# Pooled attention and mixture of depths: keys on every second partition, exponentials in four tiles, row broadcasts moved ahead

## The chip, the cores and the metric

The kernel runs on one core of a Trainium2 chip. The metric is device time in microseconds (us) of one execution, as the median of several runs. The core has five engines with a queue each: PE (TensorE, with PEld for its weight loads), DVE (VectorE), ACT (ScalarE), POOL (GpSimd) and SP (SyncE, which issues most transfers here). Each works through its own queue in order and waits for the others by semaphores.

## What is computed

The input q, k and v have shape 8 x 8 x 576 x 64 (batch, heads, tokens, head size). Keys and values are averaged over groups of 8 tokens, so each head has 72 keys:

```
k_p = k.reshape(B, H, 72, 8, D).mean(axis=3); v_p likewise
attn = softmax(q @ k_p^T / sqrt(D)); x = attn @ v_p       # x as (B, 576, 512)
scores = x @ w_gate                                       # one per token
top = the 128 tokens of each batch with the highest score
out = x; out[top] += sigmoid(scores[top]) * (relu(x[top] @ w1) @ w2)
```

w1 is 512 x 1024 and w2 is 1024 x 512. Everything is float32.

## The kernel before

All the work is in `direct_path` (`general_path` is a second way that runs only when a flag says that a softmax sum left its range, which these inputs don't do). There are 8 batches. A batch has 3 steps (`u`, 24 in all), and a step has two chunks of 96 tokens.

**Loads.** SP's queue loads k and q as 128-partition tiles (L99, L103) and v as two tiles of four heads (`load_v`, L105 to L110), with the 72 keys on partitions 0 to 71, in one transfer of 64 partitions and one of 8. Batches 0 and 1 are loaded at the start, and batch b+2 while batch b is worked on.

**Pooling.** `pool_k` (L180, L181) and `pool_v` (L197 to L201) add neighbouring tokens. They run on POOL, apart from k of batch 0 and the second v tile of batch 0, which run on DVE. `k_trans` on DVE transposes k (L186) and makes the last addition (L190). `gate_v` on DVE (L205) puts v times w_gate, summed, into one more column of the pooled v. A further column holds the constant 8, so that the attention matmul also gives the softmax sum.

**A step.** `attend` (L244, PE) multiplies the exponentials of one chunk by the pooled v, `norm` (L256 to L262, DVE) divides by the sum, `scores` (L227, PE) makes the scores of the next step into four PSUM banks, and four ACT instructions (L232) take their exponentials into one tile `et`. `q_trans` (L215, DVE) transposes q for the step after that.

**Selection and MLP of a batch.** `row_bcast` (L304 on PE, L306 on ACT) copies a batch's 576 scores to all partitions, in two halves. `count` (six of them, L316, L318 and L320 on DVE) counts for each token how many are ahead of it. `one_hot` (L325, L327, DVE) and `gather` (L334 on PE, L336 to L342 on DVE and POOL) turn the ranks into the 128 rows, fetched by an indirect transfer. `gate` (L350 to L352 on ACT, POOL, DVE), `x_trans` (L357, L359), `hidden` (L369, L371) and `finish` (L381 to L383, and the scatter L385) make the MLP and add it.

**The order** is written out by hand. The loop at L455 issues, for each step, attend, norm, slot 1, scores, slot 2, attend, norm, q_trans and slots 3 to 7. The table at L401 to L431 says which job of which batch goes in which slot. With w the step after a batch's last, the batch's row broadcasts stand in slots 4 and 6 of step w, and its counts in slot 7 of steps w, w+1 and w+2. In the same step w stand the finish parts 1 and 2 of the batch two before (slots 3 and 5), `gate` and `x_trans` of the batch before (slots 2 and 7), and the pooling of k and of the first v tile of the next batch on POOL.

Of the kernel before, what the change touches and what calls it, by code (L numbers as in the profile page):

```python
# [7 lines left out]
FT = mybir.dt.float32  # L8
# [3 lines left out]
OP = mybir.AluOpType  # L12
AX = mybir.AxisListType
# [35 lines left out]
def direct_path(ctx, tc, q, k, v, moe_w_gate, moe_w1, moe_w2, moe_capacity, out, flag):  # L49
# [49 lines left out]
    def load_q(b):  # L101
        QR[b] = work.tile([128, TG, D], FT, name="qraw")
        nc.sync.dma_start(out=QR[b], in_=q[b].rearrange("h (g t) d -> (h g) t d", g=G))  # L103

    def load_v(b, g):  # L105
        x = work.tile([SP, HG, POOLW, D], FT, name="vraw", bufs=4)
        VR[b, g] = x
        src = v[b, HG * g : HG * (g + 1)].rearrange("h (p t) d -> p h (t d)", t=POOLW)
        for lo, hi in ((0, 64), (64, SP)):
            nc.sync.dma_start(out=x[lo:hi].rearrange("p h t d -> p h (t d)"), in_=src[lo:hi])  # L110

    load_k(0)
    load_q(0)
# [2 lines left out]

    wg = const.tile([SP, H, D], FT)
    nc.scalar.dma_start(out=wg.rearrange("p h d -> p (h d)"),  # L120
                        in_=bass.AP(tensor=moe_w_gate.tensor, offset=moe_w_gate.offset, ap=[[0, SP], [1, DM]]))
# [14 lines left out]
    vps = []  # L136
    for i in range(2):
        t = const.tile([SP, H, E], FT, name=f"vp{i}")
        nc.gpsimd.memset(t[:, :, D : D + 1], float(POOLW))
        nc.gpsimd.memset(t[:, :, D + 2 : E], 0.0)  # L140
        vps.append(t)
# [41 lines left out]
    def k_trans(b):  # L183

        half = work.tile([128, 2, 2 * G, R], FT, name="kh", bufs=1)
        nc.vector.transpose(out=half.rearrange("p j c r -> p r j c"),  # L186
                            in_=KS[b].rearrange("p r (j e) -> p r j e", j=2))
        KT[b] = work.tile([128, 2, 2, SP], FT, name="kt")
        x = half.rearrange("p j c r -> p (j c r)").rearrange("p (n two) -> p n two", two=2)
        nc.vector.tensor_tensor(out=KT[b].rearrange("p j s n -> p (j s n)"), in0=x[:, :, 0], in1=x[:, :, 1],  # L190
                                op=OP.add)

    def pool_v(b, g, eng):
        x = VR[b, g]
# [24 lines left out]

    def scores(u):  # L220
        b = u // NTH
        p = [bank(i, [SP, 4, 128]) for i in range(4)]
        for s in range(2):
            for j in range(2):
                for i in range(4):
                    r = slice(32 * i, 32 * i + 32)
                    nc.tensor.matmul(p[i][:, 2 * s : 2 * s + 2, 0:C], KT[b][r, j, s, :],  # L227
                                     QT[u][r, :, j, :, G * s : G * s + G],
                                     start=(j == 0), stop=(j == 1))
        ET[u] = work.tile([SP, H * 2, G, CT], FT, name="et")  # L230
# [6 lines left out]
    def attend(a):  # L237
        u, cc = divmod(a, 2)
        b = u // NTH
        p = psum.tile([C, 2, 512], FT, name="pA")  # L240
        for h in range(H):
            g, n = divmod(h, HG)

            nc.tensor.matmul(p[:, g, E * n : E * n + E], ET[u][:, 2 * h + cc].rearrange("p g t -> p (g t)"),  # L244
                             VP[b][:, h, :], start=True, stop=True)
        PA[a] = p[:, :, 0 : HG * E].rearrange("p g (n d) -> p g n d", d=E)

# [146 lines left out]
    def at(u, slot, *job):  # L394
        jobs.setdefault((u, slot), []).append(job)
# [442 lines left out]
```

## Time and profile before

| what | value |
|---|---|
| median of 3 runs | 322.35 us (321.96 to 323.08) |
| the profiled execution's own time | 325.23 us |
| its span, first to last instruction | 323.4 us |
| PE busy | 270.0 us (83%) |
| DVE busy | 192.0 us (59%) |
| POOL busy | 147.9 us (46%) |
| ACT busy | 103.1 us (32%) |

The profile is one execution. A line of a timeline gives the start and the length of an instruction or of a merged run of them, its line in the kernel, the tile written and the tiles read, and in brackets how long the engine had waited before it and for what. A chain of waits follows the work that ended last back to what released it. Busy shares are averages over stages with different limits, so each stage is read by itself.

### The profile page before, as it was taken

Reading aid. Unit: us, or ns where it says so; the run is one execution under the profiler, and the core shown is the slowest. Engines: PE = TensorE matmul, PEld = TensorE weight load, DVE = VectorE, ACT = ScalarE, POOL = GpSimd, SP = SyncE. Lnnn points to the kernel's source line nnn. Section 1 sums busy time; section 2 is a strip of 40 time slices with the busy share of each in tenths; the row PEclk is TensorE's granted clock in tenths of the full one; section 3 lists DMA queues with packets and bytes.
Section 4 is the critical chain, followed back from the end, with each engine's and each line's share of the span. In section 5 each row is a group of like instructions: output and inputs, shape, how many; then the busy total and the mean of one; then the engine's idle time right before and its main releaser. Section 6 shows DMA issues by size and latency. Waiting matters only on the chain.

```text
span 323.4 us, 6460 instructions
## 1 busy us (share of the span) xinstructions
PE 270.0 (83%) x2562; PEld 247.6 (77%) x2562; DVE 192.0 (59%) x604; ACT 103.1 (32%) x178; POOL 147.9 (46%) x182
## 2 busy tenths in 40 slices
PE   0368769963699999979999799969996999999890
PEld 0238658853489989968998699969996899989890
DVE  0985532897358638992699439962897367383000
ACT  1150332350422444242344054404541441221210
POOL 1269408901890077907491649345862120423111
PEclk9965755595757999995999599978998799999997
DMA  7999999999692286637651937021111121201001
GB/s 248 247 225 310 221 339 309 230 262 330 118 240 79 63 239 143 210 96 207 145 206 32 264 101 228 29 82 46 40 49 51 32 83 52 82 34 32 34 0 43
DMA packets 12954, 46.78 MB, mean 145 GB/s; under 512 B 1324, under 2 KB 1324, under 8 KB 10868
## 3 DMA queue, kind: packets, MB, share of 16 engines
q1 hardware_dynamic: 11552, 41.95, 47.1%
q0 software_dynamic: 1280, 4.20, 4.2%
q8 instruction: 22, 0.36, 0.5%
q10 hardware_dynamic: 84, 0.15, 0.3%
q14 instruction: 16, 0.13, 0.1%
HBM read 34.75 MB, written 11.53 MB: 143 GB/s over the span
## 4 chain that ended last, share of the span: by engine, by line
PE 51%; DVE 32%; DMA 8%; issue 3%; POOL 2%; ACT 1%; SPq 0%; POOLq 0%; ACTq 0%
PE pA L244 18%; PE bank L381 13%; PE bank L227 9%; PE bank L369 9%; DVE cmp L320 7%; DVE cmp L318 4%; DVE cmp L316 4%; DVE xs L258 4%; DMA vraw<-in_v_dram 4%; DVE qt L215 3%; DMA xr<-out_dram,idx 3%; DVE kh L186 2%; DVE kt L190 2%; DVE oh L327 1%; DMA out_dram<-xs 1%
## 5 line engine op out<-in xcount | busy, mean ns | idle before, releaser
L232 ACT ACTIVATE et<-bank 72x384 f32<-72x384 f32 x96 | 71.1, 900 | 123.3 <-PE bank L227 123.3
L244 PEld LDWEIGHTS pA<-vp,et 72*96 72x96 f32 x768 | 88.2, 202 | 16.4 <-issue 11.2
L244 PE MATMUL pA<-vp,et 72*96 72x96 f32 x768 | 95.3, 290 | 6.4 <-DVE vp L205 3.6
L227 PE MATMUL bank<-qt,kt 32*72 32x192 f32 x768 | 53.3, 422 | 18.2 <-DVE qt L215 12.3
L369 PE MATMUL bank<-xg,w 128*128 128x128 f32 x512 | 61.4, 280 | 1.5 <-ACT xg L359 1.5
L369 PEld LDWEIGHTS bank<-xg,w 128*128 128x128 f32 x512 | 59.8, 196 | 1.9 <-ACT xg L359 1.9
L381 PE MATMUL bank<-w,ht 128*128 128x176 f32 (+1 forms) x384 | 59.5, 309 | 0.0
L383 POOL TENSOR_TENSOR y<-y,xr 128x176 f32<-128x176 f32 (+1 forms) x24 | 13.2, 551 | 97.8 <-ACT y L382 97.7
L227 PEld LDWEIGHTS bank<-qt,kt 32*72 32x72 f32 x768 | 37.1, 181 | 27.0 <-DVE qt L215 12.3
L381 PEld LDWEIGHTS bank<-w,ht 128*128 128x128 f32 x384 | 55.9, 190 | 0.0
L197 POOL TENSOR_TENSOR vraw<-vraw 72x1024 f32<-72x1024 f32 x15 | 35.4, 2361 | 12.0 <-DMA vraw<-in_v_dram 11.9
L258 DVE TENSOR_TENSOR xs<-pA,rz 96x512 f32<-96x512 f32 x48 | 33.0, 686 | 1.7
L320 DVE SCALAR_TENSOR_TENSOR cmp<-sr,sc,before 96x96 bf16<-96x96 f32 x48 | 32.1, 669 | 0.3
L318 DVE TENSOR_SCALAR_CACHE_REDUCE cmp<-sr,sc 96x576 bf16<-96x576 f32 (+5 forms) x48 | 26.6, 554 | 9.4 <-ACT sr L306 9.4
L256 DVE TENSOR_SCALAR zall<-pA 96x8 f32<-96x8 f32 x48 | 7.5, 156 | 41.2 <-PE pA L244 41.2
L371 ACT ACTIVATE ht<-bank 128x384 f32<-128x384 f32 (+1 forms) x24 | 10.9, 455 | 41.9 <-PE bank L369 41.9
L382 ACT ACTIVATE y<-bank,g 128x176 f32<-128x176 f32 (+1 forms) x24 | 9.7, 403 | 42.1 <-PE bank L381 42.1
L215 DVE STREAM_TRANSPOSE qt<-qraw 128x768 f32<-128x768 f32 x24 | 23.1, 964 | 0.0
L352 DVE RECIPROCAL g<-g 128x1 f32<-128x1 f32 x8 | 1.3, 163 | 36.1 <-POOL g L351 36.1
L316 DVE TENSOR_SCALAR_CACHE_REDUCE cmp<-sr,sc 96x96 bf16<-96x96 f32 (+4 forms) x40 | 20.2, 505 | 0.9
L180 POOL TENSOR_TENSOR kraw<-kraw 128x1152 f32<-128x1152 f32 x7 | 18.5, 2636 | 2.5 <-DMA kraw<-in_k_dram 2.5
L198 POOL TENSOR_TENSOR vraw<-vraw 72x512 f32<-72x512 f32 x15 | 19.0, 1269 | 1.2
(70 smaller groups left out, 180.7 us busy)
## 6 DMA issues: line engine op xcount, KB each, us to landing
kraw<-in_k_dram SPq DMA_DIRECT2D x8, 1152.0 KB
qraw<-in_q_dram SPq DMA_DIRECT2D x8, 1152.0 KB
out_dram<-xs SPq DMA_DIRECT2D x24, 384.0 KB
vraw<-in_v_dram SPq DMA_DIRECT2D x16, 512.0 KB
w<-in_moe_w_dram SPq DMA_DIRECT2D x2, 2048.0 KB
vraw<-in_v_dram SPq DMA_DIRECT2D x16, 64.0 KB
wg<-in_moe_w_gate_dram ACTq DMA_DIRECT2D x1, 144.0 KB
xr<-out_dram,idx POOLq DMA_INDIRECT x8, 4.8
```

The source lines that it names most:

```text
L197: eng.tensor_tensor(out=x[:, :, 0:4, :], in0=x[:, :, 0:4, :], in1=x[:, :, 4:8, :], op=OP.add)
L198: eng.tensor_tensor(out=x[:, :, 0:2, :], in0=x[:, :, 0:2, :], in1=x[:, :, 2:4, :], op=OP.add)
L215: nc.vector.transpose(out=QT[u].rearrange("p cc j t c -> p t (cc j) c"), in_=QR[b].rearrange("p (t c) d -> p t (c d)", c=NC)[:, :, 2 * D * ...
L227: nc.tensor.matmul(p[i][:, 2 * s : 2 * s + 2, 0:C], KT[b][r, j, s, :], QT[u][r, :, j, :, G * s : G * s + G], start=(j == 0), stop=(j == 1))
L232: nc.scalar.activation(ET[u][:, 4 * i : 4 * i + 4].rearrange("p n g t -> p n t g"), p[i][:, :, 0:C].rearrange("p n (t g) -> p n t g", g=G) ...
L244: nc.tensor.matmul(p[:, g, E * n : E * n + E], ET[u][:, 2 * h + cc].rearrange("p g t -> p (g t)"), VP[b][:, h, :], start=True, stop=True)
L258: nc.vector.tensor_tensor(out=XS[b][:, c, :].rearrange("p (g n d) -> p g n d", g=2, d=D), in0=o[:, :, :, 0:D], in1=rz.rearrange("p (g n on ...
L316: nc.vector.tensor_scalar(cmp[:, 0 : c * C], row[:, 0 : c * C], s, None, op0=OP.is_ge, op1=OP.add, accum_out=CN[b][:, c, 0:1])
L318: nc.vector.tensor_scalar(cmp[:, c * C : S], row[:, c * C : S], s, None, op0=OP.is_gt, op1=OP.add, accum_out=CN[b][:, c, 1:2])
L320: nc.vector.scalar_tensor_tensor(cmp[:, 0:C], row[:, c * C : c * C + C], s, before, op0=OP.is_equal, op1=OP.mult, accum_out=CN[b][:, c, 2:3])
L369: nc.tensor.matmul(p[:, n, :], w1[:, d, 128 * f : 128 * f + 128], XG[b][:, d, :], start=(d == 0), stop=(d == DB - 1))
L381: nc.tensor.matmul(p, HT[b][:, f, :], w2[:, f, c], start=(f == 0), stop=(f == FB - 1))
```

## The change

v is loaded to every second partition: keys 0 to 63 go to partitions 0, 2, ..., 126 and keys 64 to 71 to partitions 1, 17, ..., 113. The partitions between hold zeros, so the tiles that carry keys all have 128 partitions: the pooled v (`vp`), the transposed keys (`kt`, now 128 columns with zeros between), the score banks and the exponentials. The zeros are written once at the start. The column of 8s must be 8 on the partitions with a key only, so it is built from an index tile. The last addition of `k_trans` becomes two. The exponentials go to four tiles in place of one. Both row broadcasts move to slot 3 and to other banks, the finish parts 1 and 2 to slots 5 and 6, the third count to step w, and the last count and `one_hot` to slot 3.

```diff
+    vraws = [const.tile([128, HG, POOLW, D], FT, name=f"vraw{i}") for i in range(4)]
+    for i, t in enumerate(vraws):
+        (nc.vector, nc.gpsimd)[i % 2].memset(t, 0.0)
     def load_v(b, g):
-        x = work.tile([SP, HG, POOLW, D], FT, name="vraw", bufs=4)
+        x = vraws[(2 * b + g) % 4]
...
-        for lo, hi in ((0, 64), (64, SP)):
-            nc.sync.dma_start(out=x[lo:hi].rearrange("p h t d -> p h (t d)"), in_=src[lo:hi])
+        x = x.rearrange("p h t d -> p h (t d)")
+        nc.sync.dma_start(out=x[0:128:2], in_=src[0:64])
+        nc.sync.dma_start(out=x[1:128:16], in_=src[64:SP])
...
-    wg = const.tile([SP, H, D], FT)
+    wg = const.tile([128, H, D], FT)
...
+    vps = [const.tile([128, H, E], FT, name=f"vp{i}") for i in range(2)]
+    kts = [const.tile([128, 2, 2, 128], FT, name=f"kt{i}") for i in range(2)]
+    for t in kts + vps:
+        nc.gpsimd.memset(t, 0.0)
+    keys = const.tile([128, SP], FT)
+    nc.gpsimd.iota(keys[:, 0:64], pattern=[[2, 64]], base=0, channel_multiplier=-1,
...
+    nc.gpsimd.iota(keys[:, 64:SP], pattern=[[16, 8]], base=1, channel_multiplier=-1,
...
+    eights = const.tile([128, 1], FT)
+    nc.vector.tensor_scalar(keys, keys, 0.0, float(POOLW), op0=OP.is_equal, op1=OP.mult)
+    nc.vector.tensor_reduce(out=eights, in_=keys, axis=AX.X, op=OP.add)
+    for t in vps:
+        nc.vector.tensor_scalar(t[:, :, D], t[:, :, D], eights, None, op0=OP.add)
...
-        nc.vector.tensor_tensor(out=KT[b].rearrange("p j s n -> p (j s n)"), in0=x[:, :, 0], in1=x[:, :, 1],
-                                op=OP.add)
+        nc.vector.tensor_tensor(out=y[:, :, 0:128:2], in0=x[:, :, 0:64, 0], in1=x[:, :, 0:64, 1], op=OP.add)
+        nc.vector.tensor_tensor(out=y[:, :, 1:128:16], in0=x[:, :, 64:SP, 0], in1=x[:, :, 64:SP, 1], op=OP.add)
...
-        p = [bank(i, [SP, 4, 128]) for i in range(4)]
+        p = [bank(i, [128, 4, 128]) for i in range(4)]
...
-        ET[u] = work.tile([SP, H * 2, G, CT], FT, name="et")
+        ET[u] = [work.tile([128, 4, G, CT], FT, name=f"et{i}") for i in range(4)]
...
-        p = bank(2 * half + 1, [C, n, C])
+        p = bank(half, [C, n, C])
...
-        at(w, 4, row_bcast, b, 0)
-        at(w, 6, row_bcast, b, 1)
+        at(w, 3, row_bcast, b, 0)
+        at(w, 3, row_bcast, b, 1)
         for c in range(NC):
-            at(w + (0 if last else (0, 0, 1, 1, 1, 2)[c]), 7, count, b, c)
-        at(w + (0 if last else 2), 7, one_hot, b)
+            at(w + (0 if last else (0, 0, 0, 1, 1, 2)[c]), 7 if last or c < 5 else 3, count, b, c)
+        at(w + (0 if last else 2), 7 if last else 3, one_hot, b)
...
-        at(w + 6, 3, finish, b, 1, 0)
-        at(w + 6, 5, finish, b, 2, 2)
+        at(w + 6, 5, finish, b, 1, 2)
+        at(w + 6, 6, finish, b, 2, 3)
```

## Rows read from the trace of the kernel before

**Rows 1.** Chain of waits, pieces: start, length, engine, tile, line
```profile
113.08 0.97 DVE oh L327
...
144.56 0.97 DVE oh L327
...
178.77 0.96 DVE oh L327
...
190.13 2.22 PE bank L381 x16
...
193.08 0.83 DVE cmp L318 x2
...
247.09 0.96 DVE oh L327
```

**Rows 2.** Timeline of DVE in one turn (start, length; in brackets the wait before)
```profile
155.99 0.96 DVE L215 STREAM_TRANSPOSE qt<-qraw 128x768 f32<-128x768 f32 x1
...
158.90 0.81 DVE L318 TENSOR_SCALAR_CACHE_REDUCE cmp<-sr,sc 96x576 bf16<-96x576 f32 x1 [1.94 <-ACT sr L306]
...
159.75 3.34 DVE L320 SCALAR_TENSOR_TENSOR cmp<-sr,sc,before 96x96 bf16<-96x96 f32 x1
...
168.68 1.24 DVE L190 TENSOR_TENSOR kt<-kh 128x288 f32<-128x288 f32 x1
...
172.33 0.31 DVE L320 SCALAR_TENSOR_TENSOR cmp<-sr,sc,before 96x96 bf16<-96x96 f32 x1
...
176.90 0.37 DVE L205 TENSOR_REDUCE vp<-vraw 72x4 f32<-72x256 f32 x1
```

**Rows 3.** Timeline of POOL in the same turn
```profile
159.47 1.10 POOL L385 DMA_INDIRECT out_dram<-y,idx  x1 [0.29 <-POOL y L383]
160.59 2.38 POOL L197 TENSOR_TENSOR vraw<-vraw 72x1024 f32<-72x1024 f32 x1
...
168.33 1.27 POOL L198 TENSOR_TENSOR vraw<-vraw 72x512 f32<-72x512 f32 x1
```

**Rows 4.** Timeline of PE: batch 0's gather, then the same turn and the next
```profile
78.14 0.32 PE L334 MATMUL bank<-auxb,oh 96*128 96x5 bf16 x6 [6.08 <-DVE oh L327]
...
160.13 1.54 PE L227 MATMUL bank<-qt,kt 32*72 32x192 f32 x32
...
179.78 0.32 PE L334 MATMUL bank<-auxb,oh 96*128 96x5 bf16 x6 [2.44 <-DVE oh L327]
...
182.74 2.85 PE L227 MATMUL bank<-qt,kt 32*72 32x192 f32 x32
```

**Rows 5.** Busy time by stretch: us, PE, PEld, DVE, ACT, POOL, PEclk, DMA, GB/s
```profile
100.90:145.30 44.40, 41.52 (x452) 39.20 (x451) 34.11 (x110) 17.43 (x30) 19.98 (x23) 1.00 0.49 140
...
179.40:186.20 6.80, 6.42 (x58) 5.36 (x59) 2.10 (x9) 0.53 (x1) 4.89 (x8) 0.50 0.92 242
186.20:213.50 27.30, 25.18 (x264) 24.08 (x263) 21.98 (x64) 12.13 (x22) 14.61 (x14) 1.00 0.41 120
```

**Rows 6.** Timeline of ACT, the exponentials of a step
```profile
185.67 2.98 ACT L232 ACTIVATE et<-bank 72x384 f32<-72x384 f32 x4 [7.89 <-PE bank L227]
```

**Rows 7.** Busy time by stretch at the start, columns as in rows 5
```profile
6.00:8.00 2.00, 0.00 (x0) 0.00 (x0) 0.55 (x1) 0.00 (x0) 0.00 (x0) 1.00 0.99 410
...
10.00:12.00 2.00, 0.00 (x0) 0.00 (x0) 1.97 (x3) 0.00 (x0) 0.00 (x0) 1.00 1.03 199
```

**Rows 8.** Timelines of POOL and DVE at the start
```profile
1.45 0.29 POOL L140 MEMSET vp<- 72x240 f32 x1
...
21.69 2.75 POOL L180 TENSOR_TENSOR kraw<-kraw 128x1152 f32<-128x1152 f32 x1 [2.48 <-DMA kraw<-in_k_dram]
...
22.00 2.72 DVE L201 TENSOR_TENSOR vraw<-vp,wg 72x256 f32<-72x256 f32 x1
```

**Rows 9.** Groups of weight loads between 160 and 179 us (busy, mean ns)
```profile
L369 PEld LDWEIGHTS bank<-xg,w 128*128 128x128 f32 x64 | 7.3, 192 | 0.0
...
L227 PEld LDWEIGHTS bank<-qt,kt 32*72 32x72 f32 x64 | 2.4, 137 | 0.4 <-issue 0.3
```

More of the change, by code (lines that the diff above doesn't have):

```diff
@@ L115, in direct_path @@
     load_v(0, 1)
-    wg = const.tile([SP, H, D], FT)
+    wg = const.tile([128, H, D], FT)
     nc.scalar.dma_start(out=wg.rearrange("p h d -> p (h d)"),
-                        in_=bass.AP(tensor=moe_w_gate.tensor, offset=moe_w_gate.offset, ap=[[0, SP], [1, DM]]))
+                        in_=bass.AP(tensor=moe_w_gate.tensor, offset=moe_w_gate.offset, ap=[[0, 128], [1, DM]]))
     first = const.tile([C, 1], FT)
@@ L135, in direct_path @@
     nc.gpsimd.iota(chunk0, pattern=[[1, NC]], base=0, channel_multiplier=0, allow_small_or_imprecise_dtypes=True)
[L136 to L141, printed above, removed]
+    vps = [const.tile([128, H, E], FT, name=f"vp{i}") for i in range(2)]
[4 more added lines that the diff above has]
+    nc.gpsimd.iota(keys[:, 0:64], pattern=[[2, 64]], base=0, channel_multiplier=-1,
+                   allow_small_or_imprecise_dtypes=True)
+    nc.gpsimd.iota(keys[:, 64:SP], pattern=[[16, 8]], base=1, channel_multiplier=-1,
+                   allow_small_or_imprecise_dtypes=True)
     ident = const.tile([128, 128], FT)
@@ L187, in k_trans @@
                             in_=KS[b].rearrange("p r (j e) -> p r j e", j=2))
-        KT[b] = work.tile([128, 2, 2, SP], FT, name="kt")
-        x = half.rearrange("p j c r -> p (j c r)").rearrange("p (n two) -> p n two", two=2)
-        nc.vector.tensor_tensor(out=KT[b].rearrange("p j s n -> p (j s n)"), in0=x[:, :, 0], in1=x[:, :, 1],
-                                op=OP.add)
+        KT[b] = kts[b % 2]
+        x = half.rearrange("p j c r -> p (j c r)").rearrange("p (js n two) -> p js n two", n=SP, two=2)
+        y = KT[b].rearrange("p j s n -> p (j s) n")
+        nc.vector.tensor_tensor(out=y[:, :, 0:128:2], in0=x[:, :, 0:64, 0], in1=x[:, :, 0:64, 1], op=OP.add)
+        nc.vector.tensor_tensor(out=y[:, :, 1:128:16], in0=x[:, :, 64:SP, 0], in1=x[:, :, 64:SP, 1], op=OP.add)
     def pool_v(b, g, eng):
@@ L229, in scores @@
                                      start=(j == 0), stop=(j == 1))
-        ET[u] = work.tile([SP, H * 2, G, CT], FT, name="et")
+        ET[u] = [work.tile([128, 4, G, CT], FT, name=f"et{i}") for i in range(4)]
         for i in range(4):
-            nc.scalar.activation(ET[u][:, 4 * i : 4 * i + 4].rearrange("p n g t -> p n t g"),
+            nc.scalar.activation(ET[u][i].rearrange("p n g t -> p n t g"),
                                  p[i][:, :, 0:C].rearrange("p n (t g) -> p n t g", g=G), AF.Exp, scale=exp_scale)
@@ L242, in attend @@
             g, n = divmod(h, HG)
-            nc.tensor.matmul(p[:, g, E * n : E * n + E], ET[u][:, 2 * h + cc].rearrange("p g t -> p (g t)"),
+            nc.tensor.matmul(p[:, g, E * n : E * n + E], ET[u][h // 2][:, 2 * (h % 2) + cc].rearrange("p g t -> p (g t)"),
                              VP[b][:, h, :], start=True, stop=True)
```

## The prediction

> **What bounds the kernel now.** The page's busy shares put PE highest, but a share is a mean over stages, so I read the chain of waits next. From 113 us to 247 us it repeats itself once per batch, a "turn", and I count a turn from one `one_hot` (L327) to the next: 31.5, 34.2, and then two in 68.3, so 34.2 each [rows 1]. In a turn the chain stays on DVE from the first count to `one_hot`, and then goes over PE and ACT back to the first count. DVE's timeline shows the first leg without a gap: 158.90 to 179.73 (178.77 plus 0.96), 20.8 us [rows 1, 2]. The second leg, 179.73 to the next first count at 193.08, is 13.35 us [rows 1]. Together 34.2.
>
> Three losses are in that loop. First, DVE has finished `q_trans` at 156.95 and waits 1.94 us for ACT's copy of the broadcast scores [rows 2], because PE makes the second broadcast only after the two finish parts, the last of which ends at 192.35 in the next turn [rows 1]. Second, the first count's L320 takes 3.34 us where the same instruction takes 0.31 elsewhere [rows 2]. It ends just after POOL's scatter and the first pooling addition, 159.47 to 162.97 [rows 3], so DVE was held while POOL ran. Third, PE waits 2.44 us for `one_hot` [rows 4]. In the 6.8 us after that wait its granted clock is 0.50 (1.2 GHz), and in the 27.3 us that follow it is 1.00 (2.4 GHz) [rows 5]. The scores of a step take 2.85 us at the one and 1.54 at the other [rows 4]. The 44 us before 145.3 ran wholly at 1.00, with PE busy for 41.52 [rows 5].
>
> A turn's PE work is 25.18 + 6.42 = 31.6 us [rows 5]. With the second at full clock it is 25.2 + 3.2 = 28.4. That is the floor under a shorter loop.
>
> **The change, part by part.**
>
> *Row broadcasts to slot 3.* PE makes them right behind the second attention, and ACT copies them behind the exponentials. DVE, which still has to pass `gate`, `norm` and `q_trans`, finds them there: the wait of 1.94 goes wholly [rows 2]. What is late next is DVE itself. The broadcasts now pass the finish parts on PE and ACT, so y, the scatter and the first v tile's pooling on POOL come later. Finish part 1 moves to bank 2, which it gets when the third of the four exponentials is done. They need 2.98 us [rows 6], so about 2.4 after the scores, while PE has attention and broadcasts for some 2.0 (1.5 and 0.5): a wait of 0.4, taken as 0.5.
>
> *Counts.* With the first count 1.9 earlier and the scatter about 0.5 later, the first L320 meets only the short addition to y and costs 0.31 in place of 3.34: -3.0 [rows 2]. But the third count now stands in the same step. Call the first count's new start C. In the old turn the scatter started 0.57 after the first count and the pooling addition ended 4.07 after it [rows 2, 3]; now these are about C + 3.0 and C + 6.5. Two counts at 1.2 and the third's first two instructions bring DVE to its L320 at about C + 3.3, inside that stretch, so it waits some 3 us. I take the two as equal: 0, with bounds of -3 (it slips in before the scatter) and +0.5.
>
> *`one_hot` and the last count to slot 3.* The L205 in front of them, 0.3 us, goes behind: -0.3 [rows 2]. The gather follows as before.
>
> *k's last addition in two.* The one L190 took 1.24 because it waited for POOL's L198, which ended at 169.60 [rows 2, 3]. A second one costs 0.1 if it follows at once, and 1.3 if POOL's next addition of that kind gets between: +0.6 taken.
>
> First leg: 20.8 - 0 - 0.3 + 0.6 = 21.1, with bounds of 17.6 and 22.3.
>
> *The clock.* PE's wait for `one_hot` becomes 2.44 - 1.94 + 0.3 (the first leg's growth) - 0.5 (the bank) = 0.3 us. In the 44 us at full clock [rows 5] PE was idle for 2.9 us in all, so short waits did not bring it down there, and I expect no fall. Then attention and scores at the start of the second leg take 1.31 us less each (2.85 against 1.54 [rows 4], the attention taken alike): 13.35 - 1.94 - 2.6 = 8.8.
>
> Turn: 21.1 + 8.8 = 29.9, above PE's floor of 28.4 + 0.5.
>
> *Exponentials in four tiles, 128 partitions in place of 72.* The elements per partition of ACT, DVE and POOL don't change, and an attention uses exponentials of the step before, so nothing waits less: 0. The scores' weights go from 72 to 128 columns. Loads have a mean of 137 ns at 72 columns and 192 at 128 [rows 9], but 32 of them fit into a scores step of 1.54 us [rows 4], so they overlap and I take 0. If the 55 ns showed once for each group of four, 8 groups would be 0.44 us a step and 1.3 a turn: PE's floor would be 30.2, so +0.3 a turn.
>
> *v across the partitions.* While only v is on its way the transfers run at 199 GB/s, and with q and k at 410 [rows 7]. v of batch 0 is 1.18 MB, so 5.9 us, and 2.9 at the higher rate. The Trainium skill ("SBUF — State Buffer", "Door 1: The DMA port swizzle") says that partitions 0 to 63 reach 8 of 16 ports and that all 128 reach 16; by it the even partitions should run at the higher rate, and by that the start could gain up to 3 us. No row shows a transfer to every second partition, so the bounds are 0 and 2.9 saved, and I take the middle, 1.5. The gain doesn't reach the end: the first v tile pools earlier on POOL, but the second pools on DVE, and L201 there took 2.72 us beside POOL's L180 [rows 8]. With k of batch 1 landing earlier (POOL now waits 2.48 for it [rows 8]) more of DVE's additions run beside POOL. I set 0, with bounds of -1.5 and +3.
>
> *Zeros and index tiles at the start.* 240 elements took 0.29 us on POOL [rows 8], about 1.2 ns each at most, so POOL's 2 x 2048, 2 x 512 and 2 x 768 elements take up to 8 us, until about 9 us. The eights on DVE wait for that in front of k's first addition, which started at about 7.5. So up to 2 us on k's path, hidden because the first attention then waited for v until 25 us. SP's first v transfer waits for a zeroed tile; k and q, in front of it, fill those microseconds: 0.
>
> *First two batches.* PE's wait of 6.08 [rows 4] shortens by about 1, since the third count goes to an earlier step: -1.3 with batch 1's L205. *End.* Finish part 1 of batch 6 gets the bank of the last gather directly behind it, and waits for DVE to read it: +0.5.
>
> **Sum**, against the profiled execution's 325.23 us. Three turns of 34.2 at 29.9: -12.9. The turn of 31.5, which began at full clock: -1.6. The half-rate stretch after 247: -2.6. First batches -1.3, end +0.5. Together -17.9, so 307.3. The median stands 0.9% below that execution, so 322.35 - 17.7 = about 305.
>
> **Rivals.**
> - *The clock still falls.* PE's wait stays long enough, say 1 to 1.5 us, if the second k addition is held. The turn is then 21.1 + 11.4 = 32.5, the half-rate stretch after 247 stays: -5.1 - 1.6 - 1.3 + 0.5 = -7.5, so 315. For it: only a few tenths lie between, and each of the last turns' falls followed such a wait [rows 4, 5].
> - *The third count slips in* before the scatter. The first leg loses 3 and PE's floor of 28.9 binds: another 1 us on each of four turns, so about 300.
> - *Slower: POOL holds DVE more than now.* Place: k's second addition (+1.3) and a further L320 behind the second v tile's first addition (2.38 long [rows 3]), with the clock still falling. First leg 20.8 + 3.7 = 24.5, turn 35.9, and 3 at the start: 322.35 + 3 x 1.7 + 3 - 1.3, so 329. It decides from a first leg of 22.8 on. Against it: POOL's work per turn doesn't grow.
> - *Slower: the scores' weight loads queue.* 32 loads x 55 ns [rows 9] make 1.76 us on each of 24 steps, 42 us: about 347. Against it: 32 x 137 ns is 4.4 us, in a step of 1.54 [rows 4], so they don't queue. The Trainium skill ("TensorE: Matmul & The Clock Gate", "LDWEIGHTS") gives a load's time by its columns, columns / 1.2 ns, so 107 ns in place of 60. By that rule 32 loads in a row would already exceed 1.54 now, so the trace bears out the growth but not a queue.
> - *v stays at 199 GB/s*: the change wouldn't do what it says, and the time is still 305, since the gain comes from the turns.
>
> **How the numbers follow.** Forecast (full clock, 305) 0.55; clock falls (315) 0.24; third count slips in (300) 0.08; POOL holds DVE (329) 0.06; loads queue (347) 0.03; gains cancel 0.04. About 0.3%, 1 us, is what a measurement can tell. Faster 0.87, within 0.04, slower 0.09. The range of 298 to 318 takes in the first three with their bounds; the forecast's own is 300 to 310.
>
> **What would show it.** Right: no wait of L318 for `sr`; the first L320 short and the third long; a turn near 30 us; PE's wait at L334 under 1 us; granted clock 1.00 from about 100 us to the end; 2 KB transfers of v above 199 GB/s with little moved at 25 us. Wrong: half-rate stretches between 140 and 255 us; L320 or k's additions beside POOL in more places; scores steps above 1.54 us at full clock.

## The result and the profile after

The kernel after takes 300.45 us (median of 4 runs, 298.99 to 303.06), the kernel before, in the same comparison, 322.72 (4 runs, 321.96 to 323.69). The ratio is 0.9317, 95% interval 0.9238 to 0.9396. Forecast were 305 us and a range of 298 to 318: the time is 22.3 us less where 17.7 less was expected. Each ratio below is to the kernel before on the same chip and leaves out most disturbed runs, so it can differ from the quotient of the medians.

The profiled execution of the kernel after is its slowest, 303.06 us, span 301.2. From its page:

```profile
PE 251.9 (84%) x2562; PEld 236.0 (78%) x2562; DVE 198.6 (66%) x618; ACT 102.9 (34%) x178; POOL 155.8 (52%) x186
...
PEclk9999977966599999999999999999999999999997
```

PE is busy for 252 us where it was 270: the same matmuls (those with keys on more partitions), at a higher granted clock. The row PEclk shows the clock low only before 85 us and in the last slice. Busy time by stretch, columns as in [rows 5]:

```profile
83.00:136.00 53.00, 50.28 (x562) 47.30 (x556) 41.92 (x136) 24.08 (x41) 32.71 (x33) 1.00 0.47 156
136.00:196.00 60.00, 58.62 (x642) 55.23 (x641) 46.73 (x146) 25.25 (x44) 39.22 (x44) 1.00 0.54 177
196.00:298.00 102.00, 93.50 (x899) 89.37 (x897) 51.35 (x191) 30.86 (x61) 37.37 (x57) 1.00 0.16 48
```

No half-rate stretch is left between 83 and 298 us, and in the middle stretch PE is busy for 58.62 of 60 us. The timeline of PE, the gather (L353 now, L334 in [rows 4]), gives the turns:

```profile
77.75 0.32 PE L353 MATMUL bank<-auxb,oh 96*128 96x5 bf16 x6 [4.44 <-DVE oh L346]
...
107.12 0.31 PE L353 MATMUL bank<-auxb,oh 96*128 96x5 bf16 x6 [0.26 <-DVE oh L346]
...
137.17 0.30 PE L353 MATMUL bank<-auxb,oh 96*128 96x5 bf16 x6 [0.26 <-DVE oh L346]
...
167.22 0.31 PE L353 MATMUL bank<-auxb,oh 96*128 96x5 bf16 x6 [0.26 <-DVE oh L346]
```

A turn is 30.05 us, and PE's wait for `one_hot` is 0.26 where it was 2.44 [rows 4]. DVE in that turn (L337 is the old L318, L339 the old L320, L209 and L210 are k's two last additions):

```profile
147.36 0.80 DVE L337 TENSOR_SCALAR_CACHE_REDUCE cmp<-sr,sc 96x576 bf16<-96x576 f32 x1
...
148.21 0.31 DVE L339 SCALAR_TENSOR_TENSOR cmp<-sr,sc,before 96x96 bf16<-96x96 f32 x1
...
150.66 2.18 DVE L339 SCALAR_TENSOR_TENSOR cmp<-sr,sc,before 96x96 bf16<-96x96 f32 x1
...
157.10 1.20 DVE L209 TENSOR_TENSOR kt<-kh 128x256 f32<-128x256 f32 x1
158.22 1.27 DVE L210 TENSOR_TENSOR kt<-kh 128x32 f32<-128x32 f32 x1
...
166.20 0.96 DVE L346 TENSOR_TENSOR oh<-slots,rank 96x768 bf16<-96x768 f32 x1
```

The first count (147.36) has no wait for the broadcast scores, against 1.94 in [rows 2]. Its L339 is short, the third count's takes 2.18, and both of k's additions are long. POOL explains the 2.18:

```profile
150.33 2.39 POOL L216 TENSOR_TENSOR vraw<-vraw 128x1024 f32<-128x1024 f32 x1
```

That L339 ends at 152.84, just after L216 (152.72), as the first L320 did in [rows 2, 3].

Counted in the two profiled executions: up to `one_hot` of batch 1 it is 7.0 us less (113.08 to 106.11), in the turn after it 1.4, in the three turns of 34.2 together 12.4, and behind them 1.4. That makes 22.2 us, the difference of the two spans.

### The profile page after: what moved, and what is told of

Read it like the earlier page. It is cut to its first block, busy times and chain, and to the rows that moved or that the text cites. A ratio compares the mean times of both kernels' runs of the same rounds, so it can differ in the third digit from the quotient of the medians.

```text
span 301.2 us, 6544 instructions
## 1 busy us (share of the span) xinstructions
PE 251.9 (84%) x2562; PEld 236.0 (78%) x2562; DVE 198.6 (66%) x618; ACT 102.9 (34%) x178; POOL 155.8 (52%) x186
## 4 chain that ended last, share of the span: by engine, by line
PE 36%; DVE 34%; POOL 15%; issue 10%; ACT 2%; POOLq 0%; ACTq 0%
PE bank L400 11%; PE pA L263 10%; PE bank L388 7%; PE bank L246 6%; DVE xs L277 5%; DVE qt L234 5%; DVE cmp L339 5%; DVE cmp L337 3%; DVE cmp L335 3%; POOL kraw L198 3%; DVE kh L204 2%; POOL vraw L217 2%; ACT et L251 2%; POOL vraw L216 2%; DVE rz L276 2%
## 5 line engine op out<-in xcount | busy, mean ns | idle before, releaser
L251 ACT ACTIVATE et<-bank 128x384 f32<-128x384 f32 x96 | 71.3, 906 | 101.7 <-PE bank L246 101.7
L263 PE MATMUL pA<-vp,et 128*96 128x96 f32 x768 | 83.6, 267 | 11.6 <-DVE vp L224 4.6
L263 PEld LDWEIGHTS pA<-vp,et 128*96 128x96 f32 x768 | 76.9, 179 | 18.9 <-issue 11.9
L246 PE MATMUL bank<-qt,kt 32*128 32x192 f32 x768 | 46.4, 375 | 19.1 <-DVE qt L234 13.2
L388 PE MATMUL bank<-xg,w 128*128 128x128 f32 x512 | 60.0, 276 | 1.5 <-ACT xg L378 1.5
L388 PEld LDWEIGHTS bank<-xg,w 128*128 128x128 f32 x512 | 58.3, 192 | 1.9 <-ACT xg L378 1.9
L246 PEld LDWEIGHTS bank<-qt,kt 32*128 32x128 f32 x768 | 38.2, 212 | 22.9 <-issue 17.8
L216 POOL TENSOR_TENSOR vraw<-vraw 128x1024 f32<-128x1024 f32 x15 | 36.0, 2397 | 5.2 <-DMA vraw<-in_v_dram 5.1
L277 DVE TENSOR_TENSOR xs<-pA,rz 96x512 f32<-96x512 f32 x48 | 32.9, 686 | 1.7
L339 DVE SCALAR_TENSOR_TENSOR cmp<-sr,sc,before 96x96 bf16<-96x96 f32 x48 | 27.2, 566 | 0.3
L337 DVE TENSOR_SCALAR_CACHE_REDUCE cmp<-sr,sc 96x576 bf16<-96x576 f32 (+5 forms) x48 | 26.6, 554 | 0.0
L371 DVE RECIPROCAL g<-g 128x1 f32<-128x1 f32 x8 | 1.3, 164 | 34.5 <-POOL g L370 34.5
L217 POOL TENSOR_TENSOR vraw<-vraw 128x512 f32<-128x512 f32 x15 | 19.4, 1291 | 1.2
```

The source lines that it names most:

```text
L216: eng.tensor_tensor(out=x[:, :, 0:4, :], in0=x[:, :, 0:4, :], in1=x[:, :, 4:8, :], op=OP.add)
L251: nc.scalar.activation(ET[u][i].rearrange("p n g t -> p n t g"), p[i][:, :, 0:C].rearrange("p n (t g) -> p n t g", g=G), AF.Exp, scale=exp ...
L263: nc.tensor.matmul(p[:, g, E * n : E * n + E], ET[u][h // 2][:, 2 * (h % 2) + cc].rearrange("p g t -> p (g t)"), VP[b][:, h, :], start=Tru ...
L277: nc.vector.tensor_tensor(out=XS[b][:, c, :].rearrange("p (g n d) -> p g n d", g=2, d=D), in0=o[:, :, :, 0:D], in1=rz.rearrange("p (g n on ...
L337: nc.vector.tensor_scalar(cmp[:, c * C : S], row[:, c * C : S], s, None, op0=OP.is_gt, op1=OP.add, accum_out=CN[b][:, c, 1:2])
L339: nc.vector.scalar_tensor_tensor(cmp[:, 0:C], row[:, c * C : c * C + C], s, before, op0=OP.is_equal, op1=OP.mult, accum_out=CN[b][:, c, 2:3])
```

## The experiments

Twelve kernels, each timed in 4 runs or more. Eight were timed on a chip on which the kernel before had medians of 322.1 and 322.6 us; the four from "The broadcasts back" to the comparison for equal scores on another, on which its median was 321.5, with single runs from 315.8 to 324.4, so their ratios have wide intervals. The first question was which half of the change does it.

**The order alone.** The kernel before with the new job table and the new banks of the broadcasts:

```diff
-        at(w, 4, row_bcast, b, 0)
-        at(w, 6, row_bcast, b, 1)
+        at(w, 3, row_bcast, b, 0)
+        at(w, 3, row_bcast, b, 1)
...
-        p = bank(2 * half + 1, [C, n, C])
+        p = bank(half, [C, n, C])
```

(with the counts, `one_hot` and the finish parts as in the change)

> The kernel before with the new order of jobs and banks alone, v as before. Theory (the turns' gain is the order's, the gain before 107 us is v's): turns of about 29.8 us at clock 1.00; batch 0's gather still lands 9 us after its issue and the half-rate stretch after 87 us stays; so about 306 us. Rival (the order makes the whole gain, the early clock too): about 300 us, with no half-rate stretch after 87 us.

Measured: 306.0 us (303.0 to 308.2), ratio 0.951 (0.942 to 0.960). PE's wait in front of the gather is 0.24, the granted clock is 1.00 from 93 to 297 us, and the gathers of batches 1 to 5 stand at 108.90 to 227.41, so 29.63 a turn, 0.4 less than with the layout. Two of its runs took 303 to 304 us and two 308. Alone, the order gives 16 of the 22 us by the medians. In the profiled executions it gives all of it: the span is 301.3 us, and 301.2 with both halves (this one is the fastest run of its kernel, that one the slowest of its own).

**The layout alone.** The kernel after with the old job table and the old banks, the same diff the other way round.

> The changed kernel with the old order of jobs and the old banks. Theory: v at some 320 GB/s or more, first full attention at 28 us, batch 0's gather landing in about 5 us, full clock from about 83 us until the first turn's end, then turns of 34.2 us with a half-rate stretch in each; about 318 us. Rival (order alone): 322 to 326 us, since the zeros and the held additions at the start cost 3 us and nothing comes back.

Measured: 307.5 us (306.1 to 308.7), ratio 0.953 (0.946 to 0.960). Both expectations missed: the half that was thought to be worth little gives nearly as much alone, and the halves don't add up. In the profiled executions it takes 17.5 us off the span, 11.0 of them ahead of `one_hot` of batch 1 (at 102.12 in place of 113.08) and 5.9 in the four turns. Its PE timeline in the turns:

```profile
134.81 0.31 PE L353 MATMUL bank<-auxb,oh 96*128 96x5 bf16 x6 [1.94 <-DVE oh L346]
...
157.23 1.58 PE L246 MATMUL bank<-qt,kt 32*128 32x192 f32 x32 [0.71 <-DVE kt L210]
...
166.49 0.31 PE L353 MATMUL bank<-auxb,oh 96*128 96x5 bf16 x6 [1.94 <-DVE oh L346]
...
199.76 0.31 PE L353 MATMUL bank<-auxb,oh 96*128 96x5 bf16 x6 [1.95 <-DVE oh L346]
```

The second addition of k is held while POOL runs, PE waits 0.71 for it ahead of the scores, and so waits 0.5 less ahead of the gather. After the wait at 134.81 the clock stays up (turn 31.68). After the one at 166.49 it is at 0.50 for 3.4 us (turn 33.27), by stretch:

```profile
134.80:167.60 32.80, 30.14 (x335) 28.52 (x335) 24.99 (x77) 12.68 (x22) 19.66 (x23) 1.00 0.52 174
167.60:171.00 3.40, 3.40 (x32) 3.23 (x36) 1.12 (x4) 0.00 (x0) 2.82 (x7) 0.50 0.88 312
```

In the kernel before each of the four waits of 2.44 is followed by 6.8 us at 0.50. This led to a theory of the turns for both halves: what either removes is PE's stretch of idleness, with the fall of the clock behind it. Single parts came next.

**v on contiguous partitions.** The kernel after, keys on partitions 0 to 71 of tiles that keep 128 partitions:

```diff
-        nc.sync.dma_start(out=x[0:128:2], in_=src[0:64])
-        nc.sync.dma_start(out=x[1:128:16], in_=src[64:SP])
+        nc.sync.dma_start(out=x[0:64], in_=src[0:64])
+        nc.sync.dma_start(out=x[64:SP], in_=src[64:SP])
```

> The changed kernel, but keys 0 to 71 on partitions 0 to 71 of the same 128-partition tiles (zeros behind them). Theory (it is the spacing of the partitions, not the wider tiles or the const tiles, that makes v faster): v at 199 GB/s again, 2 KB packets near 165 ns, batch 0's gather near 9 us, turns still 30 us; about 306 us. Rival (the wider tiles or the order free the transfers): v above 300 GB/s, 300 us.

Measured: 302.5 us (300.7 to 304.0), ratio 0.938 (0.930 to 0.945). While only v is on its way, the kernel after moves (busy time by stretch, the last column is GB/s):

```profile
10.00:12.00 2.00, 0.00 (x0) 0.00 (x0) 1.93 (x3) 0.00 (x0) 0.00 (x0) 1.00 1.05 323
```

and with v on contiguous partitions

```profile
10.00:12.00 2.00, 0.00 (x0) 0.00 (x0) 1.93 (x3) 0.00 (x0) 0.00 (x0) 1.00 1.08 212
```

The transfers do what the diff says, 199 [rows 7] to 323 GB/s, and the time hardly depends on it: the two ranges overlap, the interval holds the ratio of the kernel after, and 2 us is what is left at most in the medians.

**The second v tile of batch 0 on POOL**, in place of DVE:

```diff
-    pool_v(0, 1, nc.vector)
+    pool_v(0, 1, nc.gpsimd)
```

> The changed kernel with the second v tile of batch 0 pooled on POOL in place of DVE. Theory (DVE's four additions were held by POOL's, which put the first full attention 3 us later than before): pooling ends at 23.1, first full attention near 23.7 in place of 28.2, everything behind it as early unless the clock changes: 296 to 297 us. Rival (the start is hidden behind later waits, on DVE or transfers): 300 us.

Measured: 302.4 us (300.2 to 305.0), ratio 0.938 (0.927 to 0.949). In the kernel after DVE's additions run beside POOL's pooling of k:

```profile
21.99 1.79 DVE L217 TENSOR_TENSOR vraw<-vraw 128x512 f32<-128x512 f32 x1
23.81 2.45 DVE L218 TENSOR_TENSOR vp<-vraw 128x256 f32<-128x256 f32 x1
26.30 1.37 DVE L220 TENSOR_TENSOR vraw<-vp,wg 128x256 f32<-128x256 f32 x1
```

and PE goes on at 28.17, against 25.23 in the kernel before. With the tile on POOL it goes on at 23.95, 4.2 earlier. In the profiled executions 3.2 of it are left at `one_hot` of batch 1 (102.91 against 106.11), but the medians don't show it, 302.4 against 300.45 with ranges that overlap. So the time does not follow the start, as far as this spread lets one tell.

**The broadcasts back** to their old slots and banks (the finish parts 1 and 2 too), the rest as after:

```diff
-        at(w, 3, row_bcast, b, 0)
-        at(w, 3, row_bcast, b, 1)
+        at(w, 4, row_bcast, b, 0)
+        at(w, 6, row_bcast, b, 1)
```

> The changed kernel with the row broadcasts and finish parts 1 and 2 in their old slots and banks; counts and one_hot stay in their new slots. Theory (the broadcasts' place is what takes DVE's wait and with it the fall of the clock): the first L337 waits some 1.9 us for sr again, L339 is held by the scatter and pooling, PE waits over 2 us at L353, the clock falls to 0.50 for 6.8 us a turn, turns near 33 to 34 us; 313 to 317 us. Rival (counts and one_hot made it): turns of 30, about 300 us.

Measured: 302.0 us (301.0 to 303.2), ratio 0.951 (0.933 to 0.969): the prediction's main step falls, the rival stands. The DVE wait that the move was to remove is there, but small, and the first L339 is held as long as in the kernel before. PE's wait in front of the gather is short all the same (DVE, then PE):

```profile
144.40 0.81 DVE L337 TENSOR_SCALAR_CACHE_REDUCE cmp<-sr,sc 96x576 bf16<-96x576 f32 x1 [0.36 <-ACT sr L325]
...
145.25 3.34 DVE L339 SCALAR_TENSOR_TENSOR cmp<-sr,sc,before 96x96 bf16<-96x96 f32 x1
```

```profile
164.59 0.30 PE L353 MATMUL bank<-auxb,oh 96*128 96x5 bf16 x6 [0.26 <-DVE oh L346]
```

The clock is 1.00 from 78.5 to 293 us and a turn takes 30.83, so the move is worth 0.8 a turn. Of the 1.94 us in [rows 2] most was not the slot's doing.

**The third count back** in the next step:

```diff
-            at(w + (0 if last else (0, 0, 0, 1, 1, 2)[c]), 7 if last or c < 5 else 3, count, b, c)
+            at(w + (0 if last else (0, 0, 1, 1, 1, 2)[c]), 7 if last or c < 5 else 3, count, b, c)
```

> The changed kernel with the third count back in step w+1. The prediction took its move as worth 0 (an L339 held for 2 us in one place, against none). Theory: DVE loses the 1.9 us of being held, but PE's work and small waits (0.7 us a turn) bound the turn: turns 29.6 to 30.0, 298 to 301 us. Rival (the move shortens the loop): turns longer by the 1.4 us of one count, the clock falling again, over 306 us.

Measured: 305.9 us (305.4 to 306.5), ratio 0.962 (0.944 to 0.979), slower than after. The held L339 is gone, and two other losses take its place (DVE's timeline):

```profile
150.50 0.16 DVE L275 TENSOR_SCALAR zall<-pA 96x8 f32<-96x8 f32 x1 [1.85 <-PE pA L263]
...
153.74 2.30 DVE L209 TENSOR_TENSOR kt<-kh 128x256 f32<-128x256 f32 x1
...
155.96 1.28 DVE L210 TENSOR_TENSOR kt<-kh 128x32 f32<-128x32 f32 x1
```

DVE waits 1.85 for PE's attention at the place where the kernel after is held for 2.18, and then comes early to k's additions and is held there 1.1 longer. PE waits longer in front of the gather:

```profile
166.18 0.31 PE L353 MATMUL bank<-auxb,oh 96*128 96x5 bf16 x6 [1.49 <-DVE oh L346]
```

A turn is 31.27 (32.88 the one time that the clock falls). The third count stands well where it is: it fills a wait. Of the three parts of the order that were taken back one at a time it costs a turn the most, 1.2 us.

**The last count and `one_hot` back** in slot 7:

```diff
-            at(w + (0 if last else (0, 0, 0, 1, 1, 2)[c]), 7 if last or c < 5 else 3, count, b, c)
-        at(w + (0 if last else 2), 7 if last else 3, one_hot, b)
+            at(w + (0 if last else (0, 0, 0, 1, 1, 2)[c]), 7, count, b, c)
+        at(w + (0 if last else 2), 7, one_hot, b)
```

> The changed kernel with the last count and one_hot back in slot 7, behind gate_v. Theory: one_hot ends 0.3 us later, PE's wait at L353 grows from 0.26 to about 0.6 us, the clock holds, turns 30.4 us; 302 us. Rival (the margin to the clock's fall is that small): half-rate stretches come back, 310 us or more.

Measured: 301.2 us (299.0 to 304.3), ratio 0.944 (0.920 to 0.969). PE's waits are 0.59 to 1.17, turns 30.4 to 31.0, no fall in them: 0.3 to 0.9 a turn, which the total can't tell from the spread.

**The comparison for equal scores with one SBUF input**, which leaves out the order among equal scores:

```diff
-        nc.vector.scalar_tensor_tensor(cmp[:, 0:C], row[:, c * C : c * C + C], s, before,
-                                       op0=OP.is_equal, op1=OP.mult, accum_out=CN[b][:, c, 2:3])
+        nc.vector.tensor_scalar(cmp[:, 0:C], row[:, c * C : c * C + C], s, None, op0=OP.is_equal, op1=OP.add,
+                                accum_out=CN[b][:, c, 2:3])
```

(each token now counts itself too, so the index of the slots starts at 1)

> The changed kernel with L339 as a comparison with a scalar that reads one SBUF tensor; it leaves out the order among equal scores. Theory (DVE is held by POOL only where it reads two SBUF tensors): every one of the 48 takes about 0.3 us also beside POOL's scatter and pooling, where 2.2 us stood; one_hot is ready before PE gets to it, the wait at L353 of 0.26 us goes, turns 29.7 us; 298 to 300 us. Rival (any DVE instruction is held while POOL runs): the third one still takes over 2 us.

Measured: 297.3 us (296.5 to 297.4), ratio 0.934 (0.917 to 0.951). None of the 48 is held: all take under 0.4 us, where the form with two SBUF inputs takes up to 2.2 beside POOL in the kernel after. Yet the turns are 30.04 as before. The hold goes on to k's addition:

```profile
120.57 2.30 DVE L209 TENSOR_TENSOR kt<-kh 128x256 f32<-128x256 f32 x1
122.79 1.27 DVE L210 TENSOR_TENSOR kt<-kh 128x32 f32<-128x32 f32 x1
```

and PE still waits only some 0.25 at a time. So in the turns of the kernel after PE is the bound, and time taken off DVE there buys nothing. The 3 us lie ahead of the turns (`one_hot` of batch 1 at 100.72 in place of 106.11). How much of them the edit makes is open: with the broadcasts back, and with the third count back, that `one_hot` stands at 101.92 and 102.62.

Four kernels then tested the clock by itself, in both directions.

**PE kept busy in the kernel before**, four gathers:

```diff
-        p = bank(2, [cap, 5])
+        p = bank(2, [cap, 512])
+        if 2 <= b <= 5:
+            for _ in range(16):
+                nc.tensor.matmul(p[:, 128:256], ident[:, :cap], ident, start=True, stop=True)
+        p = p[:, 0:5]
```

> The kernel before, with 16 matmuls of 128 columns (about 1.9 us at full clock, by the 5.55 us that 48 of them take in the hidden layer) put on PE in front of the gather of batches 2 to 5, where PE waits 2.44 us for the one-hot tile. Their result is not used; nothing else differs. Theory (PE's idle stretch in front of the gather brings the granted clock down, and the half-rate stretch behind it then delays the broadcast scores and with them the next count): PE's wait is 0.6 us, no half-rate stretch between 145 and 255 us, DVE's wait for the broadcast scores falls from 1.9 to about 0.4, turns of 31.6 in place of 34.2, four stretches of 2.6 saved, so 322.4 - 10.5 = 312. Rival (the clock falls for another reason, the wait is only a companion): turns of 34.2 stay, 322 to 324.

Measured: 314.9 us (313.8 to 315.2), ratio 0.977 (0.971 to 0.983). Work that nobody needs makes the kernel before 7.7 us faster. PE, then DVE, then the stretches:

```profile
172.49 3.73 PE L335 MATMUL bank<-ident 128*128 128x128 f32 x32
176.06 0.30 PE L338 MATMUL bank<-auxb,oh 96*128 96x5 bf16 x6
```

```profile
186.64 0.81 DVE L318 TENSOR_SCALAR_CACHE_REDUCE cmp<-sr,sc 96x576 bf16<-96x576 f32 x1 [0.37 <-ACT sr L306]
```

```profile
141.00:245.00 104.00, 103.64 (x1145) 98.88 (x1143) 75.82 (x230) 38.65 (x67) 60.98 (x74) 1.00 0.41 122
```

The clock stays at 1.00 throughout, and DVE's wait for the broadcast scores falls from 1.94 to 0.37 although their slot is the old one: the other 1.57 was the fall of the clock, seen one leg later. A turn is 32.41 and not 31.6, because the filler took 3.73 us, not 1.9 (each of its 16 matmuls has two records in the trace), and made the gather about 1 us late.

**k's last addition in two, in the kernel before:**

```diff
-        nc.vector.tensor_tensor(out=KT[b].rearrange("p j s n -> p (j s n)"), in0=x[:, :, 0], in1=x[:, :, 1],
-                                op=OP.add)
+        x = x.rearrange("p (js n) two -> p js n two", n=SP)
+        y = KT[b].rearrange("p j s n -> p (j s) n")
+        nc.vector.tensor_tensor(out=y[:, :, 0:64], in0=x[:, :, 0:64, 0], in1=x[:, :, 0:64, 1], op=OP.add)
+        nc.vector.tensor_tensor(out=y[:, :, 64:SP], in0=x[:, :, 64:SP, 0], in1=x[:, :, 64:SP, 1], op=OP.add)
```

> The kernel before, with only k's last addition cut in two (keys 0 to 63, keys 64 to 71, on the same partitions as before). Theory (the second addition is held about 0.7 us beside POOL, as in the run with the layout alone; PE spends that time waiting for the transposed keys, so its wait in front of the gather is 1.95 in place of 2.44, and the clock falls for 3.4 us or not at all in place of 6.8): turns of 31.6 to 33.3, mean 32.3, so 4 x 1.9 = 7.6 less, 315; an added instruction makes the kernel faster. Rival A (an added instruction on the path of DVE costs its time): 322.4 + 4 x 0.7 = 325. Rival B (the gain of the layout alone came from v's faster transfers and the first 100 us): 322.

Measured: 317.2 us (315.1 to 318.0), ratio 0.985 (0.977 to 0.993). An instruction more, and 5 us less; both rivals fall. PE's timeline and two stretches:

```profile
133.82 1.54 PE L229 MATMUL bank<-qt,kt 32*72 32x192 f32 x32 [0.72 <-DVE kt L193]
...
143.03 0.30 PE L336 MATMUL bank<-auxb,oh 96*128 96x5 bf16 x6 [1.95 <-DVE oh L329]
...
177.52 0.31 PE L336 MATMUL bank<-auxb,oh 96*128 96x5 bf16 x6 [1.94 <-DVE oh L329]
```

```profile
143.20:150.00 6.80, 6.80 (x62) 5.74 (x59) 1.78 (x8) 1.10 (x2) 5.41 (x9) 0.50 0.85 229
...
177.00:211.50 34.50, 31.32 (x354) 29.41 (x358) 25.74 (x80) 12.68 (x22) 20.68 (x24) 1.00 0.50 145
```

The addition cuts PE's one wait of 2.44 into 0.72 and 1.95. Two of the four waits of 1.95 are followed by a fall (6.8 and 3.4 us), two by none.

**DVE delayed in the kernel after**, in front of five `one_hot`:

```diff
+        if 1 <= b <= 5:
+            for _ in range(3):
+                nc.vector.tensor_scalar(cmp, SR[b].rearrange("p c i -> p (c i)"), SC[b][:, 0:1], None, op0=OP.is_gt,
+                                        op1=OP.add, accum_out=spare)
```

> The kernel after, with DVE kept busy by three more counting instructions (0.8 us each, 2.4 us, their result is not used) in front of the one-hot tile of batches 1 to 5. PE's wait in front of the gather becomes 0.26 + 2.4 = about 2.7 us. Theory (that wait brings the clock down): a half-rate stretch of 6.8 us behind each of the five waits, each costing 2.6 more than the delay, turns of 30.05 + 2.4 + 2.6 = 35 us, 300.5 + 5 x 5 = 325, slower than before. Rival (the delay alone is paid, the clock stays up): turns of 32.5, 312.5. Rival B (DVE has slack elsewhere in the turn and takes the delay up): 300 to 305.

Measured: 321.5 us (10 runs, 317.3 to 324.4), ratio 0.991 (0.985 to 0.996): the five delays, some 12 us, cost 21 by the medians. All five waits are followed by a fall, of 3.4 us each and not of 6.8, and turns are 33.8 to 34.6:

```profile
144.12 0.30 PE L359 MATMUL bank<-auxb,oh 96*128 96x5 bf16 x6 [2.70 <-DVE oh L352]
...
178.71 0.30 PE L359 MATMUL bank<-auxb,oh 96*128 96x5 bf16 x6 [3.27 <-DVE oh L352]
```

```profile
145.10:148.50 3.40, 3.40 (x33) 3.23 (x35) 1.14 (x5) 0.00 (x0) 2.66 (x7) 0.50 0.69 217
148.50:179.20 30.70, 27.01 (x290) 25.41 (x287) 24.04 (x74) 12.65 (x22) 16.57 (x15) 1.00 0.44 147
```

So the delay alone (312.5) is ruled out, the fastest run being 317.3, and the theory's 325 was 3.5 too high, for falls half as long as it supposed.

**PE kept busy early in the kernel after:**

```diff
+    def fill(n):
+        p = bank(0, [128, 512])
+        for _ in range(n):
+            nc.tensor.matmul(p[:, 0:128], ident, ident, start=True, stop=True)
+
+    at(2, 1, fill, 8)
+    at(2, 7, fill, 14)
+    at(4, 7, fill, 24)
```

(and 26 in front of the gather of batch 0, as above)

> The kernel after, with matmuls whose result is not used (0.116 us each) put on PE where it waits in the first 80 us: 8 and 14 of them in step 2, 24 in step 4, 26 in front of the gather of batch 0. They are shorter than the waits they stand in at full clock. Theory (of the first 80 us, too, the half-rate stretches are paid: 24 us of them between 42 and 83 us in the profiled run): most of them vanish, and the one-hot tile of batch 1 comes at about 101 to 103 in place of 106.1, so 296 to 298, and the spread between runs, 4 us for the kernel after, becomes smaller. Rival (in this stage the transfers and DVE's additions set the pace, and PE's clock is hidden): 300 to 301, or up to 304 where a filler runs at half rate and delays the attention behind it.

Measured: 299.9 us (299.3 to 300.4), ratio 0.932 (0.926 to 0.938). From 34 us on, the half-rate stretches ahead of 83 us vanish (from 19.5 to 33.5 the clock's row reads 0.50 in this execution):

```profile
34.00:73.00 39.00, 36.63 (x439) 34.05 (x438) 30.10 (x93) 15.35 (x22) 15.52 (x16) 1.00 0.89 314
73.00:107.00 34.00, 30.23 (x364) 28.24 (x362) 23.70 (x82) 11.86 (x20) 19.09 (x24) 1.00 0.53 177
```

`one_hot` of batch 1 comes at 102.8, against 106.1, and the runs lie within 1.2 us where those of the kernel after span 4.1. The median is 0.5 lower, within the spread. That fits early falls that come in some executions and not in others; they add little to the median, as the rival had it. These fillers, too, were twice as long as meant; shorter ones were not tried. No kernel that computes everything beat the kernel after by more than the spread.

**All waits together.** PE's waits in front of the gathers that begin and end the turns, in one profiled execution of each kernel (in the last row but one four kernels):

| kernel | partitions of the key tiles | wait, us | followed by 0.50 | turn, us |
|---|---|---|---|---|
| before | 72 | 2.44 | 4 of 4, for 6.8 us | 34.2 |
| before, k's addition in two | 72 | 1.95 | 2 of 4, for 6.8 and 3.4 | 31.6, with a fall 33.2 and 34.5 |
| layout alone | 128 | 1.94 | 2 of 4, for 3.4 | 31.7, with a fall 33.3 |
| third count back | 128 | 1.49 | 1 of 4, for 3.4 | 31.3, with a fall 32.9 |
| `one_hot` back | 128 | 0.59 to 1.17 | none | 30.4 to 31.0 |
| v contiguous | 128 | 0.28 to 0.86 | none | 30.05 to 30.6 |
| after, and order alone | 128, 72 | 0.26, 0.24 | none | 30.05, 29.63 |
| before, PE kept busy | 72 | 0 | 0 of 4 | 32.4 |
| after with: second v tile on POOL; broadcasts back; one-input comparison; PE kept busy early | 128 | 0.22 to 0.84 | none | 30.0 to 30.8 |
| after, DVE delayed | 128 | 2.7 to 3.3 | 5 of 5, for 3.4 | 33.8 to 34.6 |

## Why the prediction was right, and where not

*The clock: right, but not by the step that was named.* PE's wait was forecast at 0.3 and is 0.26, no fall follows, and the turn is 30.05 against 29.9. That the wait brings the clock down, and doesn't only go with it, is shown by the runs that fill it and that lengthen it. Three turns gave 12.4 of 12.9, the turn of 31.5 gave 1.4 of 1.6, and what lies behind them 1.4, where -2.6 and +0.5 had made 2.1. But "2.44 - 1.94 + 0.3 - 0.5" shortens the wait by the broadcasts' move. With the broadcasts back the wait is still 0.26; with the third count back it is 1.49, and with the last count and `one_hot` back 0.59 to 1.17. The counts' new places shorten it, of which the third's was taken as worth 0, and so the 0.3 was met by luck.

*PE's floor: 1 us too low.* It was put at 28.4. In the kernel after PE is busy for 29.36 us of a turn of 30.05, all at full clock (29.13 of 29.63 with the order alone). So PE's own work sets the turn, and not the sum of the two legs.

*The two legs: two errors that cancel, by luck.* The first leg was to be 21.1 and is 19.8 (147.36 to 167.16). The second was to be 8.8 and is 10.25 (137.11, the end of the `one_hot` before, to 147.36).

- The second leg failed at "13.35 - 1.94 - 2.6": it took off DVE's wait for the broadcast scores and the time at half clock as two things. The kernel before with PE kept busy has a second leg of 11.6, of which the filler's lateness is 1.0, so without the fall it is 10.6. The fall and 1.57 of the 1.94 are the same 2.7 us. The move to slot 3, named as the cause, adds the remaining 0.37.
- The first leg: the held third count took 2.18 and not some 3.3, so the counts gained 1.2 where 0 was taken (bounds -3 and +0.5). k's second addition cost 1.27 and not 0.6 (bound 1.3; where it isn't held it takes 0.20, not 0.1). Three other L320 of 0.4 to 0.7 became 0.31, 0.7 together, which was not foreseen.

*The first batches: the term that was mis-sized.* "First two batches -1.3" measured -7.0 in the two profiled executions. `one_hot` of batch 0 is only 0.4 earlier; the 35.96 us from there to batch 1's become 29.37. Most of that is the half-rate stretch from 87.3 to 100.9, which is gone. By their durations four groups of PE in it, of which the hidden layer is the longest, take 15.5 us, and 10.2 at full clock. The hidden layer before and after:

```profile
98.03 6.95 PE L369 MATMUL bank<-xg,w 128*128 128x128 f32 x48
```

```profile
92.13 5.55 PE L388 MATMUL bank<-xg,w 128*128 128x128 f32 x48
```

The prediction read falls of the clock in the turns alone, and none of those ahead of 113 us. Part of this is the execution that was shown: the kernel with PE kept busy, which differs from the one before only from batch 2 on, has that `one_hot` at 110.22, not at 113.08.

*The start: 0 taken, and about 0 in effect.* The first attention got 3 us later, by the bound of +3 and for its reason, DVE's additions beside POOL. It came back by a way not named: in the kernel before PE is at half clock for longer. The scores of the third step, before and after:

```profile
31.88 2.85 PE L227 MATMUL bank<-qt,kt 32*72 32x192 f32 x32
```

```profile
34.30 1.58 PE L246 MATMUL bank<-qt,kt 32*128 32x192 f32 x32 [0.80 <-DVE zall L275]
```

*The layout: 0 taken, and two effects measured.* In the turns its 128 partitions and second addition cost 0.42 each (30.05 against 29.63), 1.7 in four turns. Ahead of them it gains 1.8 in the profiled executions (`one_hot` of batch 1 at 106.11 against 107.89 with the order alone), so there the two cancel. The medians lie 5.5 apart, 306.0 and 300.45, but that rests on the order's two runs of 308; its other two, 303.0 and 303.9, are some 3 us above.

*The rivals.* "The clock still falls" had its condition, the second k addition held for 1.27, but PE's wait in front of the gather did not come of it. "The third count slips in" would have brought no 300: without the hold DVE waits 1.85 for PE at the same place. That 300 was measured comes from the first batches, not from a shorter turn. "POOL holds DVE more than now" needed a first leg of 22.8 and has 19.8. "v stays at 199 GB/s" was right in its conclusion, the time doesn't hang on it. The Trainium skill ("SBUF — State Buffer", "Door 1: The DMA port swizzle") gives twice the ports for partitions across all 128; the trace agrees in direction, 212 to 323 GB/s, a factor of 1.5. "The scores' weight loads queue" fell: a scores step at full clock takes 1.58 against 1.54 [rows 4]. The Trainium skill ("TensorE: Matmul & The Clock Gate", "LDWEIGHTS") has loads grow with their columns; 32 loads of 128 columns in place of 72 added 0.04 us here.

*Open.* What in the layout makes the early steps faster: tiles of 128 partitions or the four tiles of exponentials (neither was run alone; k's additions and the spread of v are excluded, the first by the run with it alone, the second by the contiguous v). Also why a fall lasts 6.8 or 3.4 us, why some waits of 1.5 to 1.95 have none, and why the kernel after's runs differ by 4 us.

## What to carry to other kernels

Before adding a wait and a slow stretch that follows it, ask whether the one is the other seen from the next engine: fill the idle engine with work that nobody needs, once, and see which of the two goes. Where PE waits once per turn for long enough that the granted clock then falls, shortening that wait, or cutting it into two, is worth more than the wait itself. And read the clock in the first stages too, by the duration of one matmul group that recurs, before calling them unchanged.

## What the runs showed of the hardware

- In front of the gathers of the turns, each of the nine waits of PE of 2.4 us and more was followed by a stretch at 0.50, of twelve waits of 1.5 to 1.95 us five were, and none was of those of 1.2 us or less. A 6.8 us stretch cost a turn 2.7 to 2.9 us, a 3.4 us stretch 1.6.
- With key tiles on 128 partitions each of the eight falls in the turns lasted 3.4 us, with 72 five of six lasted 6.8. And the third step's scores took 1.58 us in all ten kernels with 128, as a scores step does later at full clock, and 2.85 in all four with 72, as one does at 0.50, although the added partitions hold only zeros. The clock's own row reads 0.50 there in the kernel before, but 1.00 in the other three with 72, so at the start of the program this rests on the durations. The two go together in every run; no run has changed the partitions alone, so this is a regularity and not a cause.
